# Cutting 640 columns into 320 and 320 instead of 384 and 256: the k, q, v and output projections of an adaLN block

## The chip, the cores and the metric

The kernel runs on one core of one Trainium2 chip. The metric is the device time of one execution in microseconds (us); the time before is the median of three runs. The profile is one further execution of the same program, recorded by the hardware profiler. Its engines are PE (TensorE, matmuls), PEld (the weight loads that go ahead of matmuls), DVE (VectorE), ACT (ScalarE), POOL (GpSimd) and SP (the DMA queue). "L78" is line 78 of the kernel's source.

## What is computed

One transformer block on x of 2048 rows by 640 columns, with modulation vectors sa, ca, ga, sb, cb, gb made from a condition c. Attention is linear, with 32 heads of 20 columns and a learned feature map. Cut to what matters here:

```
h = layernorm(x) * (1 + ca) + sa
q, k, v = split(h @ wqkv)                 # 2048x640 each, 32 heads of 20
phi(t) = [softmax(t @ w_phi), softmax(-(t @ w_phi))]   # per head
o = phi(q) (phi(k)^T v) / (phi(q) sum(phi(k)) + 1e-6)
x = x + ga * (o @ wo)
h = layernorm(x) * (1 + cb) + sb
x = x + gb * (relu(h @ w1 + b1)^2 @ w2 + b2)
```

All of it is float32, and the output must be close to the float32 reference.

## The kernel before, in words

The 2048 rows are 16 tiles of 128. `w_phi` is folded into the weights of q and k at the start (`fold`, L271), so that a projection gives the argument of the softmax at once. Each float32 operand of a large product is split into a high and a low part of the faster float32r type, and a product is three matmuls: high by high, high by low, low by high (`three`, L86; `mm`, L76, whose only matmul line is L78). The reader needs two terms for what follows. The **moving operand** of a matmul streams through the array column by column; its width is the "384" or "256" in a row's shape, and it is also the width of the output. The **stationary operand**, 128x128, is loaded before by an LDWEIGHTS of its own, so each matmul has one.

A projection of one tile (`proj`, L396) has the tile of transposed, normed x as the stationary operand and the weights (128 rows by 640 columns, five such pieces for the depth of 640) as the moving one. The 640 columns don't fit one PSUM bank of 512 float32, so they are cut in two by the table `CUT` (L31), 384 and 256 columns, each half with a bank of its own from the pool "pj", which has four. One projection is thus 15 matmuls of 384 columns and 15 of 256. The same table cuts four things:

- `proj` for k, q and v, tiles pk, pq, pv;
- `k_step` (L606), which does k of tiles 0 and 1 at the start, one piece of the depth at a time;
- `to_sb` (L423), which ACT uses to copy k and q out of PSUM, and `v_out` (L417), which copies v into a tile in which each group of three heads (60 columns) has 64 columns;
- `do_wo` (L966), the product with `wo` after attention, tile pwo, 16 matmuls in each half.

The weights of v come from the host in the order `VCOLS` (L32). Its purpose is that each half of v holds whole groups of 60 columns and a part of the last 40: six groups and 24 columns in the first half, four groups and 16 columns in the second.

The order of the work is written by hand for PE in the whole attention part: `proj` k, `proj` v, the products of phi(k) with v of two earlier tiles (`do_kv`, L446), `proj` q, with transposes of x for later tiles in between. In odd tiles the q product is broken off three matmuls into its second half for two transposes (the `between` of `proj`). DVE and ACT between tile 2 and tile 13 are in part left to a scheduler with a model of its own. From tile 14 on they are written by hand too. The feed-forward part (tiles up, acc, ring) has cuts of its own, 384 and 256 (`L, R`), and doesn't read `CUT`.

Of the kernel before, what the change touches and what calls it, by code (L numbers as in the profile page):

```python
# [11 lines left out]
AF = mybir.ActivationFunctionType  # L12
# [5 lines left out]
D = 640  # L18
# [9 lines left out]
UN = [(60 * u, 60) for u in range(10)] + [(600, 40)]  # L28
NU = len(UN)
HALF = D // 2  # L30
CUT = ((0, 384), (384, D))  # L31
VCOLS = [*range(360), *range(600, 624), *range(360, 600), *range(624, D)]  # L32
EPS = 1e-5
POSTPONED = 4
WARM = 9
# [16 lines left out]
def kernel(  # L52
# [19 lines left out]
    nc = tc.nc  # L72
# [3 lines left out]
    def mm(o, terms, first=True, last=True, skip=False):  # L76
        for i, (a, b) in enumerate(terms):
            nc.tensor.matmul(  # L78
                o, a, b,
                start=first and i == 0, stop=last and i == len(terms) - 1,  # L80
                skip_group_check=skip,
            )

    def three(ah, al, bh, bl):
        return [(ah, bh), (ah, bl), (al, bh)]
# [52 lines left out]
    def tp(name):  # L138
        return psA.tile([P, 512], F32, tag="tp", name=name)
# [243 lines left out]
    def t1(j, *ds, more=None):  # L383
        if 0 in ds:
            HT[j] = ht(f"hT{j}", j)
        p = tp(f"ta{j}_{ds[0]}")
        for k, d in enumerate(ds):
            t_in(XB[j], d, p[:, 256 * k : 256 * k + 256])
        if more:
            mod_turn(more[0], p[:, 256:], 4)  # L390
        for k, d in enumerate(ds):
            t_out(cols_a, HT[j], d, f"a{j}", p[:, 256 * k : 256 * k + 256])
        DONE[:] = newest(ET_.Activation), newest(ET_.DVE)
        if more:
            mod_sum(*more)

    def proj(nm, t, between=None):
        p = pj(f"p{nm}{t}")
        j, i = divmod(t, 2)
        s = slice(i * P, (i + 1) * P)  # L400
        for h, (a, b) in enumerate(CUT):
            terms = []
            for d in range(NC):
                w = W[nm, d]
                terms += three(HT[j][:, d, 0, s], HT[j][:, d, 1, s], w[:, 0, a:b], w[:, 1, a:b])
            at, hook = 0, None
            if between and h == between[0]:
                at, hook = between[1:]
                mm(p[h][:, : b - a], terms[:at], last=False)
                hook()  # L410
            mm(p[h][:, : b - a], terms[at:], first=(at == 0))
        return p

    def do_v(t):
        v_out(t, proj("v", t))

    def v_out(t, p):  # L417
        v = vt[t % 2]
        nc.scalar.activation(v[:, 0:6, :60], p[0][:, :360].rearrange("p (g d) -> p g d", d=60), AF.Copy)
        nc.scalar.activation(v[:, 6:10, :60], p[1][:, :240].rearrange("p (g d) -> p g d", d=60), AF.Copy)  # L420
        nc.scalar.activation(v[:, 10, :24], p[0][:, 360:384], AF.Copy)
        nc.scalar.activation(v[:, 10, 24:40], p[1][:, 240:256], AF.Copy)

    def to_sb(p, t):
        for h, (a, b) in enumerate(CUT):
            nc.scalar.activation(t[:, a:b], p[h][:, : b - a], AF.Copy)
# [185 lines left out]
    def k_step(d):  # L612
        w = W["k", d]
        for t in range(2):
            s = slice(t * P, (t + 1) * P)
            for h, (a, b) in enumerate(CUT):
                mm(PP[t][h][:, : b - a], three(HT[0][:, d, 0, s], HT[0][:, d, 1, s], w[:, 0, a:b], w[:, 1, a:b]),
# [95 lines left out]
    for t in range(2, NT - 2):  # L713
# [13 lines left out]
        p = proj("v", t, (1, 0, lambda: t1(j + 1, 4)) if t == NT - 3 else None)  # L727
        if i == 0:
            do_kv(t - 2)
            do_kv(t - 1)  # L730
            if t in AFTER_KV:
                AFTER_KV[t]()
        v_out(t, p)
        if norm and not i:
            next(parts)
# [231 lines left out]
    def do_wo(j, i, h, a=0, b=16):  # L967
# [4 lines left out]
        s = slice(i * P, (i + 1) * P)  # L972
        cs_, n = slice(*CUT[h]), CUT[h][1] - CUT[h][0]
        terms = []
# [158 lines left out]
    for j in range(NB):  # L1133
# [53 lines left out]
        if j == 7:  # L1187
            t2(0, 4)
            p = tp("gbt")[:NC, :P]
# [513 lines left out]
```

## Time and profile before

| | us |
|---|---|
| median of 3 runs | 766.42 (765.6 to 767.21) |
| the profiled execution, whole | 766.05 |
| its span, first to last instruction | 764.3 |
| PE busy | 758.5 |
| DVE busy | 593.9 |
| ACT busy | 435.6 |
| POOL busy | 144.9 |

The granted TensorE clock is 1.000 in the whole span. Stages: up to about 34 us the weights are loaded and folded, with k of tiles 0 and 1; up to about 272 us projections and phi(k)^T v; up to about 391 us the division and the product with `wo`; behind that the feed-forward part.

A row of a group reads: line, engine, operation, output tile<-input tiles, stationary rows*columns, moving shape, count | busy us in all, mean ns of one | idle time of the engine before. A row of the timeline reads: start in us, length in us, engine, line, operation, tiles, shape and how many instructions were merged in it. Matmuls overlap in the pipeline, so the mean ns of one is its time from start to end and not the distance to the next. The distance is got from a timeline row of n equal matmuls: from its length the last one's own time is taken off, and the rest is divided by n - 1.

### The profile page before, as it was taken

To read this page: it belongs to the slowest core of one execution; us is meant where nothing else is said; L and a number is where in the kernel's file an instruction comes from. 1 tells how busy PE (TensorE), PEld (TensorE's weight loads), DVE (VectorE), ACT (ScalarE), POOL (GpSimd) and SP (SyncE) were. 2 spreads that over 40 slices of the span, in tenths; PEclk is the share of its full clock that TensorE was granted. 3 is DMA by queue.
4 is the path that set the end of the run, shared out by engine and by line. 5 is a ranking of instruction groups with operands and counts; after the bars stand their busy time and mean duration, and the time that the engine had idled before them with its cause. 6 is when DMAs were issued, how large, how long until landed. Compare 5 with 4: busy or idle time off the path is not lost.

```text
span 764.3 us, 15303 instructions
## 1 busy us (share of the span) xinstructions
PE 758.5 (99%) x5968; PEld 739.7 (97%) x5968; DVE 593.9 (78%) x1083; ACT 435.6 (57%) x972; POOL 144.9 (19%) x301
## 2 busy tenths in 40 slices
PE   9999999999999999999999999999999999999997
PEld 8999999999999989988999999999999999999997
DVE  6598897988999899999655667876767666685666
ACT  5766756677853364546776647465563645536331
POOL 3001101001100255432101000231321313213110
PEclk9999999999999999999999999999999999999999
DMA  8811431343332345223366466996766759767460
GB/s 322 329 61 78 138 104 54 104 136 112 126 104 93 109 150 188 72 87 104 122 194 221 120 227 236 283 334 209 224 166 207 232 179 268 199 184 204 126 184 35
DMA packets 51505, 126.69 MB, mean 166 GB/s; under 512 B 6684, under 2 KB 7457, under 8 KB 51433
## 3 DMA queue, kind: packets, MB, share of 16 engines
q1 hardware_dynamic: 34098, 84.65, 32.8%
q0 software_dynamic: 14752, 35.76, 16.9%
q10 hardware_dynamic: 2583, 5.30, 1.8%
q8 instruction: 47, 0.77, 0.5%
q14 instruction: 25, 0.20, 0.1%
HBM read 95.70 MB, written 29.89 MB: 164 GB/s over the span
## 4 chain that ended last, share of the span: by engine, by line
PE 91%; DVE 7%; DMA 1%; issue 0%; SPq 0%; ACT 0%; DVEq 0%
PE up L78 24%; PE acc L78 18%; PE pq L78 9%; PE pk L78 9%; PE pv L78 9%; PE pwo L78 6%; PE acc3x L78 5%; PE kvp L450 3%; PE te L920 1%; DVE dn L878 1%; DVE scr L876 1%; DVE ezb L900 1%; PE tb L357 1%; PE ta L357 1%; DVE ot L88 1%; PE foldq L280 1%
## 5 line engine op out<-in xcount | busy, mean ns | idle before, releaser
L78 PE MATMUL up<-h,w 128*128 128x256 f32 x1640 | 206.4, 278 | 0.0
L78 PEld LDWEIGHTS up<-h,w 128*128 128x128 f32 x1640 | 196.1, 188 | 0.0
L1255 ACT ACTIVATE ft<-up,b_t 128x256 f32<-128x256 f32 x104 | 49.1, 472 | 113.8 <-PE up L78 113.2
L78 PE MATMUL acc<-w,ra 128*128 128x384 f32 x452 | 97.4, 335 | 0.0
L1256 DVE TENSOR_TENSOR ft<-ft 128x256 f32<-128x256 f32 x104 | 44.1, 424 | 48.4 <-ACT ft L1255 46.8
L78 PE MATMUL pwo<-wo,ot 128*128 128x256 f32 (+3 forms) x512 | 80.5, 312 | 0.1
L78 PEld LDWEIGHTS pwo<-wo,ot 128*128 128x128 f32 (+1 forms) x512 | 74.4, 188 | 3.2 <-issue 2.7
L78 PE MATMUL pq<-wq,hT 128*128 128x384 f32 (+1 forms) x480 | 75.2, 312 | 0.0
L78 PEld LDWEIGHTS acc<-w,ra 128*128 128x128 f32 x452 | 72.7, 188 | 0.8 <-DVE ra L88 0.5
L78 PE MATMUL pk<-wk,hT 128*128 128x384 f32 (+1 forms) x480 | 72.7, 308 | 0.0
L78 PE MATMUL pv<-wv,hT 128*128 128x384 f32 (+1 forms) x480 | 71.7, 307 | 0.0
L78 PEld LDWEIGHTS pq<-wq,hT 128*128 128x128 f32 x480 | 71.1, 188 | 0.6 <-issue 0.2
L78 PEld LDWEIGHTS pk<-wk,hT 128*128 128x128 f32 x480 | 70.5, 188 | 0.4 <-issue 0.2
L78 PEld LDWEIGHTS pv<-wv,hT 128*128 128x128 f32 x480 | 70.1, 188 | 0.0
L88 DVE TENSOR_TENSOR ra<-ft,ra 128x384 fp32r<-128x384 f32 (+2 forms) x86 | 36.8, 449 | 32.6 <-ACT ra L1279 19.3
L1365 POOL DMA_DIRECT2D ring_a<-td_a x34 | 18.3, 539 | 126.1 <-PE acc L78 100.4
L1279 ACT ACTIVATE ra<-ft 128x384 fp32r<-128x384 f32 x48 | 25.2, 526 | 28.4 <-DVE ft L1256 22.4
L78 PE MATMUL acc3x<-w,ra 128*128 128x256 f32 x231 | 39.8, 278 | 0.0
L78 PEld LDWEIGHTS acc3x<-w,ra 128*128 128x128 f32 x231 | 37.2, 188 | 0.2 <-DVE ra L88 0.2
L1270 DVE TENSOR_TENSOR ft<-ft 128x128 f32<-128x128 f32 x136 | 33.4, 287 | 1.2
L441 DVE TENSOR_REDUCE sk<-ek 128x64 f32<-128x1280 f32 x16 | 23.7, 1484 | 12.4 <-ACT ek L436 10.8
L884 POOL TENSOR_TENSOR dn<-dn,rs_q 128x32 f32<-128x32 f32 x32 | 20.2, 630 | 66.7 <-DVE dn L878 66.4
(270 smaller groups left out, 1412.6 us busy)
## 6 DMA issues: line engine op xcount, KB each, us to landing
ring_c<-td_c POOLq DMA_DIRECT2D x34, 384.0 KB, 4.2
ring_a<-td_a POOLq DMA_DIRECT2D x34, 384.0 KB, 4.1
ring_b<-td_b POOLq DMA_DIRECT2D x34, 256.0 KB, 4.0
esp<-eq SPq DMA_DIRECT2D x12, 640.0 KB, 3.0
el<-esp SPq DMA_DIRECT2D x12, 640.0 KB, 3.9
rw<-in_w SPq DMA_DIRECT2D x23, 320.0 KB, 2.9
wm<-in_w_mod SPq DMA_DIRECT2D x20, 320.0 KB, 3.3
xb<-in_x SPq DMA_DIRECT2D x8, 640.0 KB, 4.2
```

What stands on the lines that cost most here:

```text
L78: nc.tensor.matmul(o, a, b, start=first and i == 0, stop=last and i == len(terms) - 1, skip_group_check=skip,)
L88: (eng or nc.vector).tensor_tensor(out_lo, full, hi.bitcast(F32), op=ALU.subtract)
L280: nc.tensor.matmul(p[g // 3][:, (g % 3) * 120 : (g % 3) * 120 + n], r, bd_t[:120, g * 120 : g * 120 + n], start=True, stop=True,)
L357: nc.tensor.transpose(p[:, i * P : (i + 1) * P], xn[:, i, d * P : (d + 1) * P], ident)
L441: nc.vector.tensor_reduce(s, heads(flat(e)), axis=AX.X, op=ALU.add)
L450: nc.tensor.matmul(kvp[g // 4][64 * c : 64 * c + 64, a : a + 2 * n].rearrange("p (s n) -> p s n", s=2), v[:, u], e[:, :, o : o + n], start ...
L884: nc.gpsimd.tensor_tensor(dn[:, s], dn[:, s], rs[:, 1 - s], op=ALU.mult)
L1255: nc.scalar.activation(r, p, AF.Relu, bias=b1_t[:, f : f + 1])
L1256: nc.vector.tensor_tensor(r, r, r, op=ALU.mult)
L1270: nc.vector.tensor_tensor(t[:, o], t[:, a], t[:, b], op=op)
L1279: nc.scalar.activation(a[:, 0, :3], t[:, :3], AF.Copy)
L1365: nc.gpsimd.dma_start(RING[j, n, r], TD[n][r].bitcast(F32R))
```

## The change

Both halves get 320 columns. `VCOLS` now puts five groups of 60 columns and 20 of the last 40 into each half of v, and `v_out` copies five groups and 20 columns of each half. Nothing else is edited; the number of matmuls, weight loads, copies and DMAs is the same.

```diff
-CUT = ((0, 384), (384, D))
-VCOLS = [*range(360), *range(600, 624), *range(360, 600), *range(624, D)]
+CUT = ((0, HALF), (HALF, D))
+VCOLS = [*range(300), *range(600, 620), *range(300, 600), *range(620, D)]
...
     def v_out(t, p):
         v = vt[t % 2]
-        nc.scalar.activation(v[:, 0:6, :60], p[0][:, :360].rearrange("p (g d) -> p g d", d=60), AF.Copy)
-        nc.scalar.activation(v[:, 6:10, :60], p[1][:, :240].rearrange("p (g d) -> p g d", d=60), AF.Copy)
-        nc.scalar.activation(v[:, 10, :24], p[0][:, 360:384], AF.Copy)
-        nc.scalar.activation(v[:, 10, 24:40], p[1][:, 240:256], AF.Copy)
+        for h in range(2):
+            nc.scalar.activation(v[:, 5 * h : 5 * h + 5, :60], p[h][:, :300].rearrange("p (g d) -> p g d", d=60), AF.Copy)
+            nc.scalar.activation(v[:, 10, 20 * h : 20 * h + 20], p[h][:, 300:320], AF.Copy)
```

On PE the order of instructions stays as it is; only widths change. This is the q product of tile 3 before, from the last matmuls of its first half (pq_0) to the two transposes (L357, into ta_4) in its second half (pq_1) and on; each row is one piece of the depth, three matmuls:

```order
L78 MATMUL pq_0_1102<-wq_419,hT_234 128x384 x3
L78 MATMUL pq_1_1103<-wq_325,hT_234 128x256 x3
L357 MATMUL ta_4_1122<-ident,xb_447 128x128 x2
L78 MATMUL pq_1_1103<-wq_336,hT_234 128x256 x3
L78 MATMUL pq_1_1103<-wq_351,hT_234 128x256 x3
```

The same place on PE in the changed kernel:

```order
L78 MATMUL pq_0_1102<-wq_419,hT_234 128x320 x3
L78 MATMUL pq_1_1103<-wq_325,hT_234 128x320 x3
L357 MATMUL ta_4_1122<-ident,xb_447 128x128 x2
L78 MATMUL pq_1_1103<-wq_336,hT_234 128x320 x3
L78 MATMUL pq_1_1103<-wq_351,hT_234 128x320 x3
```

Every first half has become 64 columns narrower and every second half 64 wider, and the transposes stand behind 18 matmuls of the product as before.

On ACT, the copies of v of tile 0 (`v_out`, from the PSUM tiles pv_0 and pv_1 into vt_104) and the first one of tile 1, before:

```order
L419 ACTIVATE vt_104<-pv_0_717 128x6x60
L420 ACTIVATE vt_104<-pv_1_718 128x4x60
L421 ACTIVATE vt_104<-pv_0_717 128x24
L422 ACTIVATE vt_104<-pv_1_718 128x16
L419 ACTIVATE vt_105<-pv_0_753 128x6x60
```

And the same place on ACT in the changed kernel:

```order
L420 ACTIVATE vt_104<-pv_0_717 128x5x60
L421 ACTIVATE vt_104<-pv_0_717 128x20
L420 ACTIVATE vt_104<-pv_1_718 128x5x60
L421 ACTIVATE vt_104<-pv_1_718 128x20
L420 ACTIVATE vt_105<-pv_0_753 128x5x60
```

Both copies of the first half now stand ahead of those of the second. In tiles 2 to 13 the scheduler also puts some neighbours on ACT and DVE in another order (the two exponentials of a tile change places, a reciprocal goes a few rows later); no instruction is added or lost.

## The prediction

> **What bounds the kernel now.** I read the page's busy times first, then its chain, then the busy times by stage, and last single streams of matmuls in the timeline. The page's first part and the chain by engine:
>
> ```profile
> PE 758.5 (99%) x5968; PEld 739.7 (97%) x5968; DVE 593.9 (78%) x1083; ACT 435.6 (57%) x972; POOL 144.9 (19%) x301
> PE 91%; DVE 7%; DMA 1%; issue 0%; SPq 0%; ACT 0%; DVEq 0%
> ```
>
> PE is busy for 99% of the span and carries 91% of the chain that ended last. But a busy PE is a share, and what matters is whether it is so in the stages that the change touches. The view of busy time by stage, whose columns are the stretch, its length, and busy time with the count of instructions for PE, PEld, DVE, ACT and POOL, then the granted clock:
>
> ```profile
> 0.00:34.00 34.00, 32.64 (x315) 31.03 (x316) 18.95 (x52) 21.18 (x46) 9.06 (x40) 1.00 0.96 354
> 34.00:63.00 29.00, 29.00 (x234) 28.87 (x232) 28.37 (x37) 20.72 (x50) 2.32 (x6) 1.00 0.22 83
> 63.00:240.00 177.00, 177.00 (x1396) 175.57 (x1395) 159.24 (x204) 116.78 (x263) 16.41 (x26) 1.00 0.33 109
> 240.00:272.00 32.00, 32.00 (x258) 29.33 (x256) 29.57 (x38) 14.20 (x39) 7.46 (x17) 1.00 0.33 103
> 272.00:391.00 119.00, 118.69 (x884) 107.70 (x883) 102.56 (x153) 69.51 (x150) 42.34 (x83) 1.00 0.35 117
> ```
>
> From 34 to 272 us, where the projections stand, PE is busy to the last hundredth; from 272 to 391 us, with the product with `wo`, 0.31 us are idle; the clock is granted in full everywhere. DVE, the next engine, has 159.24 of 177 us. So the stages go at PE's pace, and the time follows the distance from one matmul to the next. A change of that distance goes into the time one for one: if it shrinks, DVE has 10% of room; if it grows, the others only get slack.
>
> **How far matmuls stand apart.** Which matmuls are concerned and how many, from the groups kept apart by shape (the tile names are those of the four products; the 120-row forms are the last piece of the product with `wo`):
>
> ```profile
> L78 PE MATMUL pk<-wk,hT 128*128 128x384 f32 x240 | 46.5, 339 | 0.0
> L78 PE MATMUL pq<-wq,hT 128*128 128x384 f32 x240 | 46.1, 342 | 0.0
> L78 PE MATMUL pv<-wv,hT 128*128 128x384 f32 x240 | 44.3, 335 | 0.0
> L78 PE MATMUL pwo<-wo,ot 128*128 128x384 f32 x240 | 45.5, 340 | 0.1
> L78 PE MATMUL pwo<-wo,ot 120*128 120x384 f32 x16 | 5.4, 339 | 0.0
> L78 PE MATMUL pv<-wv,hT 128*128 128x256 f32 x240 | 30.2, 278 | 0.0
> L78 PE MATMUL up<-h,w 128*128 128x256 f32 x1640 | 206.4, 278 | 0.0
> ```
>
> That is 240 + 240 + 240 + 240 + 16 = 976 matmuls of 384 columns, and as many of 256: 976 pairs. The mean ns in these rows is the pass through a pipeline, not the pace. The pace stands in the timeline: 15 matmuls of 384 columns (a v product), 27 of 256 (the first feed-forward product), and two of 512 in a row (the subtraction at L960) with the one behind them:
>
> ```profile
> 72.44 2.76 PE L78 MATMUL pv<-wv,hT 128*128 128x384 f32 x15
> 389.76 3.22 PE L78 MATMUL up<-h,w 128*128 128x256 f32 x27
> 287.23 0.39 PE L960 MATMUL numa<-ot,neg 128*128 128x512 f32 x1
> 287.46 0.40 PE L960 MATMUL numb<-ot,neg 128*128 128x512 f32 x1
> 287.70 0.40 PE L960 MATMUL numc<-ot,neg 128*128 128x256 f32 x2
> ```
>
> - 384 columns: (2.76 - 0.335) / 14 = 173.2 ns.
> - 256 columns: (3.22 - 0.278) / 26 = 113.2 ns.
> - 512 columns: 287.70 - 287.23 = 0.47 us for two, 235 ns each, within some 7 ns because starts are rounded.
>
> The three don't lie on a line through zero: per column it is 0.442, 0.451 and 0.459 ns, so a wide matmul is dearer per column than a narrow one. Each further 128 columns cost 60.0 ns (173.2 - 113.2; up to 512 it is 62, within the rounding), yet the first 256 cost 113.2 and not 120. The simplest reading is blocks of 128 columns, each taking b, with a break s between one block and the next of the same matmul: 2b + s = 113.2 and 3b + 2s = 173.2 give b = 53.2 and s = 6.8 ns. Then 512 columns would be 4b + 3s = 233.2, beside the 235 that was read.
>
> The Trainium skill (TensorE: Matmul & The Clock Gate, section "Back-to-back issue gap") gives the distance at full clock as N / 2.4 + 2.5 ns. That would be 109.2, 162.5 and 215.8 ns for the three widths; the trace is above it by 4, 11 and 19 ns, so it doesn't hold for these matmuls, and the more columns, the less. By it both layouts would cost 271.7 ns a pair, and the time would stay.
>
> **The change part by part.**
>
> *The pairs.* Before, one pair costs 173.2 + 113.2 = 286.4 ns. No matmul in the trace has 320 columns. Its nearest rows are those of 256 and of 384, equally far. From above: a width between blocks may be charged as the next full one, 173.2 ns, 346.4 a pair. From below: 113.2 for 256, and 64 more columns at the pace within a block, 64 / 128 x 53.2 = 26.6, so 139.8 ns, 279.6 a pair; less would need columns that stream faster than in any row. Between these I take what the blocks say: 320 columns are two full blocks and a half one, with a break ahead of the second and one ahead of the third: 2.5 x 53.2 + 2 x 6.8 = 146.6 ns, 293.2 a pair. That is 6.8 ns more, simply because the old cut had one break and two, and the new one has two and two. Times 976: **+6.6 us**.
>
> *The copies out of PSUM.* ACT's copies by shape:
>
> ```profile
> L426 ACT ACTIVATE k<-pk 128x384 f32<-128x384 f32 x16 | 7.8, 489 | 14.0 <-PE pk L78 13.9
> L426 ACT ACTIVATE k<-pk 128x256 f32<-128x256 f32 x16 | 6.2, 384 | 13.3 <-PE pk L78 13.3
> L419 ACT ACTIVATE vt<-pv 128x360 f32<-128x360 f32 x16 | 7.5, 469 | 13.4 <-PE pv L78 9.1 <-PE kvp L450 4.3
> L420 ACT ACTIVATE vt<-pv 128x240 f32<-128x240 f32 x16 | 5.9, 371 | 8.2 <-PE pv L78 8.2
> ```
>
> Two copies of 320 cost about (489 + 384) / 2 = 436 ns each, the same sum; so do the copies of v, (469 + 371) / 2 = 420 each. Only the second copy ends 436 - 384 = 52 ns later behind its matmuls. I cost it at nothing: the next product goes on in the two other banks of the four meanwhile. If that cover were gone it would be 52 ns in 64 products (three projections and the output, 16 tiles each), 3.3 us, and would show as idle time of PE, which there is none of now.
>
> *Places that move.* In the q product of odd tiles the transposes stand behind 18 matmuls: before at 15 x 173.2 + 3 x 113.2 = 2.94 us into it, now at 18 x 146.6 = 2.64, 0.30 us sooner. Ahead of them PE has no idle time in the row of 63 to 240 us, so what they need was there; if it came late, five such tiles would lose 1.5 us at most. The same matmuls in the same order are behind them. The reordered neighbours on ACT and DVE lie beside 976 slower pairs; nothing for them.
>
> The sum: 766.05 + 6.6 = 772.65 against the profiled execution, whose 764.3 us of span leave 1.75 us around it that don't change. The median of the runs is 0.37 us higher, so it would be 773.0 from there. I forecast **772.7 us**.
>
> **The rivals.**
>
> *No change.* The columns in all are the same, and if the cost between 256 and 384 goes up evenly, 60.0 ns for 128, then 320 costs 143.2 and two of them 286.4: nothing gained, nothing lost, 766.1 us. The change then doesn't do anything to the pace. For it: three widths on one line fit an even rise as well as steps. Against it: a line that gives 6.8 ns less than nothing at zero columns has no simple cause, while breaks between blocks have one. The rule of the Trainium skill above also ends here, for another reason.
>
> *Faster.* The break may be charged only ahead of a full block, so that the half block at the end of 320 columns comes free of it: 2.5 x 53.2 + 6.8 = 139.8, the lower bound, 6.8 ns less a pair, -6.6 us, 759.4 us. It decides on one thing: whether a third, half-filled block pays the break. All three widths are whole blocks, so no row speaks against it; but a break that comes before a block can hardly know how long that block is.
>
> *Slower by more, by the pattern.* The same matmuls don't always keep the better pace. Twelve matmuls of a k product and 13 of a v product, both in the middle of their streams:
>
> ```profile
> 68.42 2.28 PE L78 MATMUL pk<-wk,hT 128*128 128x384 f32 x12
> 135.32 1.70 PE L78 MATMUL pv<-wv,hT 128*128 128x256 f32 x13
> ```
>
> (2.28 - 0.339) / 11 = 176.5 and (1.70 - 0.278) / 12 = 118.5 ns: 3.3 and 5.3 more than the streams above, with the same operands' shapes. So how the weight load and the moving operand meet makes a difference, and the change touches that: the second half now starts 320 columns into its row of weights, two and a half blocks, where it started three blocks in. If that puts all second halves into the worse pattern, some 4.3 ns x 976 = 4.2 us come on top: 776.9 us.
>
> *Slower by much.* If 320 columns are charged as 384, it is 60.0 ns a pair, 58.6 us, 824.6 us. For it speaks only that no odd width was seen.
>
> **How the numbers follow.** Breaks as I read them: 56%. The worse pattern on top: 13%. Charged as 384: 6%. No change: 14%. Faster: 11%. The range leaves out the last case above and the faster one, 17% together, and takes in no change with the runs' own scatter and the worse pattern with 2 us to spare: 764.9 to 779.0 us. A measurement of this kernel can tell about 0.2%, 1.5 us, from no change: faster 11%, the same 14%, slower 56 + 13 + 6 = 75%.
>
> **What would show it.** In the profile after, a stream of 15 matmuls of 320 columns must stand 146.6 ns apart, in first and second halves alike; 143.2 would be the even rise, 139.8 the free half block, about 151 in second halves alone the pattern, and 173 the full charge. PE must still be busy without a gap from 34 to 272 us; idle time ahead of matmuls behind ACT's copies, or ahead of the transposes, would mean that a cover failed. The feed-forward part, from the end of the product with `wo` on, must take as long as before (764.3 - 391 us). The prediction falls if pairs don't cost the same wherever they stand, or if the start of products, where PE's first matmuls wait for the pipeline, changes with the width.

## The result, and the profile after

The changed kernel takes 769.87 us (median of ten runs, 768.74 to 771.0) against 766.39 us (765.6 to 768.73) for the kernel before: ratio 1.0042, 95% interval 1.0031 to 1.0053, some 3.5 us slower. The forecast was 772.7 us, the profiled execution of before (766.05) and 6.6 us more. The profiled execution took 770.05 us, its span 768.4.

The page's busy times of the changed kernel, and its busy times by stage in the columns of the prediction:

```profile
PE 762.7 (99%) x5968; PEld 744.6 (97%) x5968; DVE 593.8 (77%) x1083; ACT 435.6 (57%) x972; POOL 143.8 (19%) x301
34.00:63.00 29.00, 29.00 (x216) 28.80 (x216) 27.91 (x36) 20.54 (x48) 1.32 (x5) 1.00 0.22 81
63.00:240.00 177.00, 177.00 (x1398) 175.08 (x1396) 157.15 (x202) 116.25 (x264) 17.03 (x28) 1.00 0.32 104
240.00:272.00 32.00, 32.00 (x250) 30.61 (x249) 29.64 (x39) 12.67 (x36) 5.33 (x12) 1.00 0.35 111
272.00:391.00 119.00, 118.90 (x883) 107.72 (x882) 104.42 (x152) 70.22 (x152) 43.84 (x86) 1.00 0.35 120
```

PE has 4.2 us more (762.7 against 758.5); DVE and ACT have what they had. PE is still busy without a gap where the projections stand, so the time that came in is PE's own. The groups of the four products after, 1952 matmuls of one width:

```profile
L78 PE MATMUL pk<-wk,hT 128*128 128x320 f32 x480 | 73.8, 310 | 0.0
L78 PE MATMUL pq<-wq,hT 128*128 128x320 f32 x480 | 75.8, 313 | 0.0
L78 PE MATMUL pv<-wv,hT 128*128 128x320 f32 x480 | 73.0, 309 | 0.0
L78 PE MATMUL pwo<-wo,ot 128*128 128x320 f32 x480 | 77.9, 313 | 0.0
L78 PE MATMUL pwo<-wo,ot 120*128 120x320 f32 x32 | 9.9, 310 | 0.0
```

And the pace, from 28 matmuls of a v product in the timeline, first and second half together:

```profile
87.50 4.27 PE L78 MATMUL pv<-wv,hT 128*128 128x320 f32 x28
```

(4.27 - 0.309) / 27 = 146.7 ns: the forecast said 146.6, the even rise 143.2, the free half block 139.8. The pair costs 293.3 ns, and against 286.7 before that is 6.5 us for 976 pairs. Half of it doesn't arrive. To see where it went, I took the distance from the start of each of these 1952 matmuls to the next matmul's start on PE, in both traces, and sorted it: what it would be at the better pace (113.3, 173.3, 146.7 ns); what lies above that by up to 12 ns, which is the slower pattern of the prediction; and what lies above by more, which are the starts of streams behind transposes and other products, and a few waits.

| us, sum over 1952 distances | before | after | difference |
|---|---|---|---|
| at the better pace | 279.8 | 286.3 | +6.5 |
| slower pattern (1881 and 1884 distances) | 2.6 | 0.2 | -2.4 |
| starts and waits (71 and 68 distances) | 7.0 | 6.2 | -0.9 |
| all | 289.5 | 292.7 | +3.2 |

The +3.2 us agree with the medians. The spans of the two profiled executions differ by 4.0 us; of the other 0.8, 0.4 came before the first k product, the loading stage, as its first matmul shows, before and after:

```profile
22.96 0.61 PE L78 MATMUL pk<-wk,hT 128*128 128x384 f32 x2
```
```profile
23.36 0.41 PE L78 MATMUL pk<-wk,hT 128*128 128x320 f32 x1
```

and about as much in the feed-forward part, where this one execution has a wait of 0.4 us for a DMA:

```profile
L78 PE MATMUL acc<-ring_c,ra 128*128 128x384 f32 x102 | 23.3, 337 | 0.4 <-DMA ring_c<-td_c 0.4
```

### The profile page after: what moved, and what is told of

Read it like the earlier page. It is cut to its first block, busy times and chain, and to the rows that moved or that the text cites. A ratio compares the mean times of both kernels' runs of the same rounds, so it can differ in the third digit from the quotient of the medians.

```text
span 768.4 us, 15304 instructions
## 1 busy us (share of the span) xinstructions
PE 762.7 (99%) x5968; PEld 744.6 (97%) x5968; DVE 593.8 (77%) x1083; ACT 435.6 (57%) x972; POOL 143.8 (19%) x301
## 4 chain that ended last, share of the span: by engine, by line
PE 98%; DMA 1%; DVE 0%; issue 0%; ACT 0%; POOL 0%; POOLq 0%
PE up L78 24%; PE acc L78 17%; PE pwo L78 10%; PE pq L78 9%; PE pk L78 9%; PE pv L78 9%; PE acc3x L78 5%; PE kvp L449 3%; PE te L919 3%; DMA ring_c<-td_c 1%; PE tb L357 1%; PE numa L78 1%; PE foldk L280 1%; PE numc L78 1%; PE numb L78 1%; PE ta L357 1%
## 5 line engine op out<-in xcount | busy, mean ns | idle before, releaser
L78 PE MATMUL acc<-w,ra 128*128 128x384 f32 x452 | 97.4, 335 | 0.0
L78 PE MATMUL pwo<-wo,ot 128*128 128x320 f32 (+1 forms) x512 | 81.2, 313 | 0.0
L78 PE MATMUL pq<-wq,hT 128*128 128x320 f32 x480 | 75.8, 313 | 0.0
L78 PE MATMUL pk<-wk,hT 128*128 128x320 f32 x480 | 73.8, 310 | 0.0
L78 PE MATMUL pv<-wv,hT 128*128 128x320 f32 x480 | 73.0, 309 | 0.0
```

Source lines behind the costliest of these rows:

```text
L78: nc.tensor.matmul(o, a, b, start=first and i == 0, stop=last and i == len(terms) - 1, skip_group_check=skip,)
```

## The experiments

My theory after the result: breaks between begun blocks set the pace (+6.5 us), and the halves of 320 win back 3.3 us because their streams don't have the slower pattern (2.4 us) and start cheaper (0.9 us). Its rivals: the cost rises evenly or goes by places in memory; the missing 3 us went elsewhere; the pattern left because the second halves lie at another address, not because of the width.

**Widths by themselves.** Behind the last product, streams of 18 float32r matmuls, one width each:

```diff
     last_downs(NB - 1)
+    for n, at in ((128, 0), (192, 0), (240, 0), (256, 0), (260, 0), (288, 0), (320, 0), (320, 64), (320, 320),
+                  (352, 0), (380, 0), (384, 0), (384, 64), (256, 64), (400, 0), (448, 0), (512, 0)):
+        for i in range(18):
+            nc.tensor.matmul(UP[:, :n], W1[2][:, i % 2, i % NC], W2[1][:, i % 2, at : at + n],
+                             start=i == 0, stop=i == 17, skip_group_check=True)
```

> The kernel before, with 17 streams of 18 float32r matmuls added behind its last product, each stream of one width, into a PSUM bank that nothing reads. The output stays the reference's. What counts is the distance from one matmul to the next within a stream. Theory (a break of 6.7 ns ahead of each further block of 128 columns that is begun, 53.3 ns per full block): 256 columns 113.3 ns, 260 121.7, 288 133.3, 320 146.7, 352 160.0, 380 171.7, 384 173.3, 400 186.7, 448 206.7, 512 233.3; 320 the same whether its moving operand starts at column 0, 64 or 320, and 256 and 384 the same from column 64. Rival 1 (the cost rises evenly with the columns): 260 115.2, 288 128.3, 320 143.3, 352 158.3, 400 180.8, 448 203.3. Rival 2 (the break belongs to fixed places in memory, every 512 bytes): 256 and 384 columns from column 64 would cost another 6.7 ns or lose one, 320 from column 64 and from column 320 would differ from that from column 0. Below 256 columns the weight load of each matmul, some 109 to 112 ns where it sets the pace in the trace of before, should keep 128, 192 and 240 columns at about 110 ns in place of 53.3, 86.7 and 106.7.

The timeline within each stream (a shape's own mean time, which is taken off once as in the prediction, is 281, 283, 296, 309, 322, 336, 336, 345, 364 and 395 ns for these widths):

```profile
767.39 2.05 PE L1647 MATMUL up<-w,w 128*128 128x256 f32 x16
769.51 2.08 PE L1647 MATMUL up<-w,w 128*128 128x260 f32 x16
771.55 2.56 PE L1647 MATMUL up<-w,w 128*128 128x288 f32 x18
774.10 7.79 PE L1647 MATMUL up<-w,w 128*128 128x320 f32 x52
782.03 2.88 PE L1647 MATMUL up<-w,w 128*128 128x352 f32 x17
784.92 2.94 PE L1647 MATMUL up<-w,w 128*128 128x380 f32 x16
788.04 6.10 PE L1647 MATMUL up<-w,w 128*128 128x384 f32 x34
796.28 3.28 PE L1647 MATMUL up<-w,w 128*128 128x400 f32 x17
799.78 3.40 PE L1647 MATMUL up<-w,w 128*128 128x448 f32 x16
803.45 4.13 PE L1647 MATMUL up<-w,w 128*128 128x512 f32 x17
```

That gives 117.9, 119.8, 133.2, 146.7, 159.9, 173.6, 174.7, 183.4, 202.4 and 233.4 ns. From 288 to 352 columns the break of the third block is paid in full, as the theory has it (133.3, 146.7, 160.0), and the even rise (128.3, 143.3, 158.3) falls. The row of 320 has three streams in it, from columns 0, 64 and 320, at one pace, and the row of 384 two, from columns 0 and 64; 256 columns from column 64 kept 117.8 ns, beside 117.9 from column 0. So the rival of fixed places falls too. But the theory is not exact at the edges: 260 columns pay some 5 of the 6.7 ns, 380 cost as much as 384 at its better pace, and of a fourth block only about half the break is paid at 400 and a third at 448 (186.7 and 206.7 were expected). And 256 and 384 columns by themselves were in the slower pattern, 117.9 in place of 113.3 and 174.7 in place of 173.3. The narrow streams of 128, 192 and 240 columns went at 111 to 112 ns, as expected if the weight load sets their pace; three widths at one pace fit that, though nothing here changed the weight load itself.

**A cut at 380.** `CUT = ((0, 380), (380, D))`, with `VCOLS` and `v_out` to match (six groups of 60 and 20 columns, then four and 20): only 4 columns change sides.

> The kernel before with the cut at 380 columns in place of 384: only 4 of 640 columns change sides. Theory (a begun block pays its whole break): the second half of 260 columns pays a second break, 121.7 ns against 113.3, the first half 171.7 against 173.3, together 293.3 a pair against 286.7, as with two halves of 320; between +3.2 us (if the slower pattern goes away as it did at 320 and 320) and +6.5 us (if it stays), so 769.6 to 772.9 us. Rival (the break is paid in the share in which the block is filled): 4 of 128 columns cost some 0.2 ns of break, the pair stays within 0.5 ns of 286.7, and the time within 0.5 us of before.

769.65 us beside 766.65 for the kernel before on the same chip, ratio 1.0038 (1.0026 to 1.0051). Twelve matmuls of a first half and 13 of a second, of one k product:

```profile
52.79 2.25 PE L78 MATMUL pk<-wk,hT 128*128 128x380 f32 x12
55.52 1.72 PE L78 MATMUL pk<-wk,hT 128*128 128x260 f32 x13
```

With 338 and 283 ns for the last, 173.8 and 119.8 ns: the pair costs what two halves of 320 cost. Four columns over the edge of a block are enough for the whole loss of the change; the proportional rival, half a microsecond, falls. All streams of 380 and of 260 keep one pace here, so nothing is left of the slower pattern, and the loss is 3 us and not 6.5. At 260 columns alone a break and a pattern that never leaves can't be told apart, as 256 columns in the slower pattern also go at up to 120.0 ns (below); that a begun block pays its break rests on the streams of 288 to 352 columns.

**One product at a time.** Halves of 320 for the product with `wo` alone (a cut of its own in `do_wo`), and for v alone (one in `proj`, with `VCOLS` and `v_out` of the change):

> The kernel before with halves of 320 in the product with wo alone; k, q and v keep 384 and 256. Theory (breaks up, slower pattern and start waits down, by the sums of distances in the two traces): 1.7 us more for 256 further breaks, 0.9 less pattern and 0.6 less at starts, +0.2 us, 766.6 us, not to be told from before. Rival (breaks alone matter, and the 3 us that are missing from the forecast went elsewhere): +1.7 us, 768.1 us.

> Halves of 320 for v alone; k, q and the product with wo keep 384 and 256. v is the product with the least of the slower pattern before (0.3 us), so it has the least to win back. Theory: 1.6 us more for 240 further breaks, 0.3 less pattern, starts as they were: +1.3 us, 767.9 us. Rival (the loss is spread evenly over the four products): 240 of 976 pairs of +3.2 us, +0.8 us, 767.4 us; the profile's sum of distances of v must tell the two apart, since the times may not.

`wo` alone: 767.26 beside 766.65 us, ratio 1.0008 (0.9999 to 1.0017). v alone: 767.6 beside 766.57, ratio 1.0014 (1.0005 to 1.0023). In the sums of distances `wo` alone adds 0.6 us and v alone 1.1. So breaks alone (1.7 us) are ruled out for `wo`, though it lost more than the theory's 0.2 us: the pattern gave back 0.7 us and not 0.9, the starts 0.4 and not 0.6. By the sums its 256 pairs, which had more of the pattern and of the starts than v's, lose less than v's 240; the times alone, with these intervals, don't show that. For v the run lies between 1.3 and the even share of 0.8 and doesn't tell them apart.

**The halves in the other order.** `CUT = ((0, 256), (256, D))`, with `VCOLS` and `v_out` to match.

> The kernel before with its two halves in the other order, 256 columns and then 384. The number of blocks and of breaks is that of before. Theory (breaks decide): the clean pace is that of before, 113.3 + 173.3 = 286.7 a pair, and only the share of the slower pattern and the waits at starts can move: 766.6 us within 1.5 us. Rival (what costs in the changed kernel is where the second half begins in its row, no more at column 384): some 770 us, as with 320.

766.34 beside 766.57 us, ratio 1.0 (0.9991 to 1.0009). The same numbers of breaks give the same time, with the second half at another place in its row. The rival falls as far as a start at a whole block goes; starts off a block were the streams of 320 from columns 64 and 320 above.

**Where the operands lie.** The transposed x, and with it the attention output, which lies in the same tiles, is moved by 128 bytes in even tiles and by 384 in odd ones. Its distance to the moving operand (the difference of their start addresses, modulo 512 bytes) goes from 192 to 320 in both: 192 + 128, and 192 - 384 is the same modulo 512. This was run first under the cut of before, then in the changed kernel:

```diff
-    def ht(name, j, at=(32, 0)):
+    def ht(name, j, at=(0, 96)):
```

> The kernel before with its cut of 384 and 256, and only the place of the transposed x in SBUF moved (by 128 bytes in even tiles, 384 in odd ones; the same for the attention output's tiles), so that the stationary operand lies at another distance from the moving one. Question: the slower pattern (176.5 and 118 ns in place of 173.3 and 113.3), which the halves of 320 no longer show. Theory A (the pattern belongs to widths and to how a stream starts, not to addresses): pace and time as before, within 0.2%. Theory B (the pattern comes from where the two operands lie to one another; the change moved that for every second half): the share of the slower pattern changes, down to none (-2.6 us, 763.8 us) or up to all streams (some +6 us, 772 us).

> The changed kernel (halves of 320) with the transposed x moved in SBUF, as in the run that moved it under the cut of 384 and 256. There the move put every 256 into the slower pattern, took 384 out of it, and cost 1.1 us. Theory A (320 is free of the pattern by its width): no difference to the changed kernel, 769.9 us within 1 us. Theory B (by its addresses): some streams of 320 fall into a slower pattern, 1 to 4 us more, 771 to 774 us.

With 384 and 256 it costs: 767.79 beside 766.65 us, ratio 1.0015 (1.0006 to 1.0024), and the sum of the slower pattern is 4.2 us where it was 2.6. All of it now sits in the 256 (4.3 ns each), none in the 384 (0.2). So addresses do have a part in the pattern: theory A of that run falls. With halves of 320 it costs nothing: 769.74 us beside 769.87 for the changed kernel, both against the same kernel before (ratios 1.0049 and 1.0042), and the pattern's sum is 0.1 us. 320 is free of it at both places.

**Eight places in one run.** Streams of 256, 320 and 384 columns at the end, with the stationary operand shifted by 64 bytes from one to the next, and the same again with the places in the opposite order:

```diff
     last_downs(NB - 1)
+    for n in (256, 320, 384):
+        for off in range(0, 128, 16):
+            for i in range(18):
+                nc.tensor.matmul(UP[:, :n], W1[2][:, i % 2].rearrange("p k n -> p (k n)")[:, off + P * (i % 4) : off + P * (i % 4) + P],
+                                 W2[1][:, i % 2, :n], start=i == 0, stop=i == 17, skip_group_check=True)
```

> The kernel before with 24 streams of 18 float32r matmuls behind its last product, into a bank that nothing reads; the output stays the reference's. Three widths, 256, 320 and 384 columns, and for each eight places of the stationary operand, 64 bytes apart, so that its distance to the moving operand, taken modulo 512 bytes, goes through 256, 192, 128, 64, 0, 448, 384, 320. Question: does the slower pattern go by this distance, and is 320 free of it at every distance? Theory A (320 is free of it because of its width): 320 keeps 146.7 ns at all eight places, 256 goes between 113.3 and 118 and 384 between 173.3 and 176.5 from place to place. Theory B (320 in the changed kernel was free of it because its second halves lie elsewhere): 320 shows distances of 149 ns or more at some of the places. Theory C (the distance has no part in it): each width keeps one pace at all places.

> The 24 streams again, with the eight places in the opposite order, so that each stream follows another one than before. If the distance alone sets the pace, each place gives the pace of the first time: 256 columns 113.4 ns at 256 bytes and 117.8 to 120.0 elsewhere, 384 columns 173.3 to 176.7 as before, 320 columns 146.7 everywhere. If the stream ahead or the start decides, 256 and 384 give other values at the same places, while 320 still gives 146.7.

The groups by shape of the first run (144 matmuls of each width, eight places together):

```profile
L1647 PE MATMUL up<-w,w 128*128 128x384 f32 x144 | 25.3, 336 | 0.0
L1647 PE MATMUL up<-w,w 128*128 128x320 f32 x144 | 21.3, 308 | 0.0
L1647 PE MATMUL up<-w,w 128*128 128x256 f32 x144 | 17.1, 281 | 0.0
```

Busy time less the last one's, by 143: 174.6, 146.8 and 117.6 ns in the mean. By place, as the mean of a stream's 17 distances, 320 kept 146.4 to 146.8 ns at all eight in both runs; 256 went between 113.3 and 120.1, 384 between 173.0 and 176.7. The width of 320 is free of the pattern at every place tried. But a place is not all: with 128 bytes between the operands modulo 512, 256 columns were slow in the first run and at the better pace in the second:

```profile
764.21 1.93 PE L1647 MATMUL up<-w,w 128*128 128x256 f32 x15
```
```profile
770.27 1.98 PE L1647 MATMUL up<-w,w 128*128 128x256 f32 x16
```

(1.93 - 0.281) / 14 = 117.8 and (1.98 - 0.279) / 15 = 113.4 ns. What went ahead of a stream matters as well. Each of these streams was profiled once. But the pattern repeats from execution to execution where nothing is changed: in the run with `wo` alone its sums for k, q and v are within 0.01 us of those of before.

**A place that would beat both?** At 256 and 128 bytes between the operands, streams of both old widths had been seen at the better pace. So the cut of before was run with x's tiles moved to these distances (it is 192 before), the feed-forward part left as it was. This is the edit for 256 bytes:

```diff
-        t = mem.tile([P, NC * 512 + (32, 96)[j % 2]], F32R, tag=f"h{j % 2}", name=name, bufs=1)
+        t = mem.tile([P, NC * 512 + (32, 112)[j % 2]], F32R, tag=f"h{j % 2}", name=name, bufs=1)
...
-    mem.tile([P, 48], F32, tag="gap", name="gap", bufs=1)
+    mem.tile([P, 32], F32, tag="gap", name="gap", bufs=1)
...
-            H2[j] = ht(f"h2_{j}", j, (0, 96))
+            H2[j] = ht(f"h2_{j}", j, (16, 112))
```

> The cut of before, 384 and 256, with the transposed x and the attention output's tiles moved by 64 bytes, so that moving and stationary operand of the four products lie 256 bytes apart modulo 512 and not 192; the feed-forward part keeps its 192. In the streams with nothing else around them, 256 bytes was the one distance at which 256 and 384 columns both kept the better pace (113.4 and 173.4 ns). Theory (distance sets the share of the slower pattern in the kernel too): most of the 2.6 us of it go, 764 us, faster than both kernels. Rival (what a stream started behind decides, and the distance only in the streams by themselves): the sum of the pattern stays at some 1.3 ns a matmul, 766.5 us.

> As the run with 256 bytes between the operands in the four products, and the same distance also in the first feed-forward product (1640 matmuls of 256 columns, tile up), whose sum of the slower pattern before is only 0.7 us. Theory: another 0.5 us, 763.5 us. Rival: no difference to the run with the four products alone.

> The cut of before, with the transposed x and the attention output's tiles moved by 64 bytes the other way, so that the operands of the four products lie 128 bytes apart modulo 512; the feed-forward part keeps its 192. At 256 bytes apart the kernel was 2.6 us slower, though the streams by themselves had been clean there, so the distance modulo 512 alone is not the law. Question: is there a place that gives 384 and 256 their better pace throughout, which would beat both kernels? Theory A (192, the place of before, is the best of those 64 bytes apart): the sum of the slower pattern is above its 2.6 us, the time above 766.5 us. Theory B (128 is one of the clean places of the second run of the streams, 113.3 and 173.2 ns): the pattern goes, 764 us.

All three are slower: 769.07 beside 766.51 us (ratio 1.0036, 1.0023 to 1.0049); 782.95 (1.0216, 1.0202 to 1.023), with the first feed-forward product moved too; and 771.03 beside 766.08 at 128 bytes (1.006, 1.0046 to 1.0074). The end of one v product, before and with 256 bytes:

```profile
88.92 1.64 PE L78 MATMUL pv<-wv,hT 128*128 128x256 f32 x13
```
```profile
89.78 1.60 PE L78 MATMUL pv<-wv,hT 128*128 128x256 f32 x12
```

(1.64 - 0.278) / 12 = 113.5 against (1.60 - 0.282) / 11 = 119.8 ns. The sums of the slower pattern are 6.5 and 7.4 us, at 256 and 128 bytes, where before has 2.6; moving the first feed-forward product as well put its 1640 matmuls at 6.0 ns above their pace (0.4 before). That is not all of its loss. The second feed-forward product (tiles acc) has both operands where they were, and yet its matmuls are slower; their largest group in that run is

```profile
L78 PE MATMUL acc<-w,ra 128*128 128x384 f32 x452 | 99.6, 340 | 0.0
```

where before has 97.4 us and 335 ns. The sum of distances of all acc matmuls goes from 177.6 to 183.3 us, with 0.4 us of it a wait for a DMA. Their streams of 9 to 12 matmuls stand between streams of the first product, and inside these streams the matmuls are 5.1 ns above their pace, where before they were 0.1. In the last stream, of 44 matmuls with nothing of the first product behind it, the first three stand 121, 121 and 116 ns apart and the following ones 113 to 114, the better pace. So a slow stream can also slow its neighbours, whose operands haven't moved. Of the four distances tried in the kernel (128, 192, 256 and 320 bytes) 192 is the best, and no version beat the kernel before.

The sums of distances and the times, side by side (differences to the kernel before, us; the times against its median on the same chip):

| cut and place | better pace | pattern | starts | sum | time |
|---|---|---|---|---|---|
| 320/320, the change | +6.5 | -2.4 | -0.9 | +3.2 | +3.5 |
| 320/320, x moved | +6.5 | -2.5 | -0.9 | +3.1 | +3.2 |
| 320/320 in `wo` alone | +1.7 | -0.7 | -0.4 | +0.6 | +0.6 |
| 320/320 in v alone | +1.6 | -0.5 | -0.1 | +1.1 | +1.0 |
| 256/384 | 0 | -0.2 | +0.4 | +0.1 | -0.2 |
| 384/256, x moved | 0 | +1.6 | -0.3 | +1.3 | +1.1 |
| 384/256, 256 bytes | 0 | +3.8 | -0.6 | +3.2 | +2.6 |
| 384/256, 128 bytes | 0 | +4.7 | -0.6 | +4.1 | +5.0 |

In every row the time follows the sum of PE's distances within 0.9 us. The column of the starts moves by -0.6 to +0.4 us also where no width changes, so the -0.9 of the change can't be put down to the width; the -2.4 of the pattern can, as 320 columns are free of it at every place. (380/260 is left out because its pace at the edges isn't the model's; its sum is +3.5 us and its time +3.0.)

## Why the prediction was right, and where its size was off

- *What bounds.* Right: the stages go at PE's pace, and the table above shows the time following the distances.
- *Blocks and breaks.* Right to 0.1 ns for 320 columns; the streams of 288 to 352 columns show the mechanism, and the cut at 380 agrees. It was read from three widths that are whole blocks, and is only roughly right for four columns of a third block and for a part of a fourth.
- *The term of +6.6 us.* This is the step that was mis-sized. "Before, one pair costs 173.2 + 113.2 = 286.4 ns" took the better pace for all pairs, though the prediction had found slower streams in the same trace. Over all distances a pair before cost 289.5 us / 976 = 296.6 ns, starts included, and after 292.7 / 976 = 299.9: 3.3 ns more, not 6.8. The breaks are there in full; 2.4 us of slower pattern and 0.9 us at the starts, which the trace of before had, are not there after. The prediction had named both as what would bring it down ("if pairs don't cost the same wherever they stand, or if the start of products ... changes with the width"), but put neither into the sum.
- *The rival of the pattern* had the sign wrong. It had the second halves fall into the slower pattern because they begin elsewhere; in fact no half of 320 has it, at any place tried. That was a property of the width, and no row of before showed that width.
- *ACT's copies, the moved transposes, the reordered neighbours* cost nothing, as forecast: PE has no idle time ahead of them, and the copies of 320 columns take 435 ns where 436 were worked out:

```profile
L425 ACT ACTIVATE k<-pk 128x320 f32<-128x320 f32 x32 | 13.6, 435 | 28.3 <-PE pk L78 28.2
```

- *The range*, 764.9 to 779.0 us, held no change as well, so that the time fell in it shows little; the pace of 146.7 ns is what bears the mechanism out.
- *No change, faster, charged as 384* are out: 146.7 ns is neither 143.2 nor 139.8 nor 173.2.

Open: what makes the slower pattern. The runs show that it depends on the width, on the two operands' places in SBUF and on what went ahead of the stream, and not on the distance modulo 512 bytes alone; whether it is this distance that counts or the place of the one operand that was moved, they don't separate. At its worst it puts 256 columns at 120.0 ns, just one break above 113.3; that it is a further break wasn't tested. Why 320 never shows it wasn't found, nor how much of the starts' gain is the width's: a start lies 98.9 ns above the pace before and 90.5 after, but also 92.4 with the old widths at 256 bytes.

## What to carry to other kernels

Where matmuls follow each other without a gap, read the pace of each width from the timeline and work in whole blocks: a cut of 640 float32r columns at 384 costs less than one at 320 or at 380, though the columns in all are the same. But sum a stage's cost over all its distances before multiplying a difference: the best stream of a trace is not its mean, and a change of shape can take away a disturbance along with what it adds. Whether a stream keeps its better pace can hang on 64 bytes of its operands' place, and on the streams around it, so a place that is good now has to be tested again after each change of layout.

## What the runs showed of the hardware that was not expected

- A move of 64 bytes of one operand in SBUF, with the same instructions, made the kernel 2.6 us slower, and of the other way 5.0; with the first feed-forward product moved as well it was 16.4 us, over 5 of them in the second one, whose operands hadn't moved.
- 256 columns go at 113.3 to 120.1 ns and 384 at 173.0 to 176.7 by place and history, but 320 columns at 146.4 to 146.8 at each of eight places.
- 128, 192 and 240 columns go at 111 to 112 ns, so below 256 columns a narrower matmul saves next to nothing when each has a weight load of its own.
